# Block-sorted attention followed by a bilinear FFN: head pairs in row and column tiles, wide loads, a hand-written TensorE order, and x transposed by the DMA crossbar

## The chip, the cores and the metric

The kernel runs on one core of a Trainium2 chip. The metric is device time in microseconds, start to end. The kernel before takes 337.42 us (median of 3 runs, 336.62 to 338.02).

Engines are named as the profile names them: PE is TensorE (matmuls), PEld its weight loads, DVE VectorE, ACT ScalarE, POOL GpSimd (here mostly the issuer of casting loads: float32 in DRAM, bf16 on the chip), SP SyncE (issuer of stores and of crossbar transposes). PSUM is the memory that matmuls write to and that the other engines copy out of. A crossbar transpose is a DMA that transposes a tile on its way (DMA_TRANSPOSE in the profile). The granted clock is the share of full speed that PE is allowed.

## The reference, cut to what matters

```python
# q, k, v: [4 batches, 8 heads, 768, 64]; sort_net: [4, 8, 8, 8]
P = sort_net
for _ in range(5):                                   # Sinkhorn: rows, then columns
    P = exp(P - max(P)); P = P / (sum(P, -1) + 1e-9); P = P / (sum(P, -2) + 1e-9)
k_sorted = einsum('bhij,bhjcd->bhicd', P, k_b)       # mixes the 8 blocks of 96 rows
v_sorted = einsum('bhij,bhjcd->bhicd', P, v_b)
scores   = q_b @ k_sorted_b.T / sqrt(64)             # within each block of 96
attn     = softmax(scores) @ v_sorted_b              # [4, 8, 768, 64]
x   = attn.transpose(0, 2, 1, 3).reshape(3072, 512)
out = ((x @ w_a) * (x @ w_b)) @ w_out                # d_ff 1536; out 3072 x 512, float32
```

Arithmetic on the chip is bf16 with fp32 accumulation.

## The kernel before

One head at a time. Both k and v of a head go through one mixing matmul per 128 rows: the stationary operand is 128 x (64 of k + 64 of v), the moving one a 128 x 128 matrix `s_all` that spreads the 8 x 8 mixing matrix over the blocks.

```python
# loads: runs of 64 elements (256 bytes), cast to bf16, issued by POOL
for t, srct in enumerate((k, v)):
    sap = _ap(srct, (b * H + h) * S * D,
              [[D, CPG], [BLK * D, NB], [CPG * D, NCH], [1, D]])
    nc.gpsimd.dma_start(out=kv_b16[:, :, t, :], in_=sap)
# mixing: k and v of one head side by side, 128 columns
nc.tensor.matmul(mix_ps[:, ch, :], lhsT=kv_b16[:, half * 3 + ch, :, :],
                 rhs=s_all[:, bh, :], start=True, stop=True)
# ... copies to kvsT, v transposed on PE, then per half head:
#     scores -> exp (ACT) -> output matmul -> reciprocal and multiply (DVE) into x_b
# at the end of a batch: x transposed on PE, 2 x (96 x 128) to a PSUM tile, and copied
for i in range(NB):
    for fc2 in range(KA // 2):
        xt_ps = ps_big.tile([P, 2, BLK], BF16, tag="psb")
        # ... two transposes, then a copy to xT by DVE (i even) or ACT (i odd)
# mask times mixing matrix, for all 32 heads, on POOL
for g in range(4):
    nc.gpsimd.tensor_tensor(out=_ap(s_all, g * 8 * P, ...), in0=..., in1=..., op=ALU.mult)
# order of the source; the scheduler interleaves it
attention_batch(0, ...)
# ... the three weights are loaded here
for b in range(B):
    if b + 1 < B:
        attention_batch(b + 1)
    ffn_ab(2 * b); ffn_ab(2 * b + 1); ffn_out(2 * b); ffn_out(2 * b + 1)
```

The softmax here doesn't subtract the row's maximum and nothing guards it: scores larger than these inputs give would overflow.

Of the kernel before, what the change touches and what calls it, by code (L numbers as in the profile page):

```python
# [12 lines left out]
INT32 = mybir.dt.int32  # L13
# [11 lines left out]
def kernel(  # L25
# [12 lines left out]
    P = 128  # L38

# [4 lines left out]
    NTOK = B * S  # L44
# [4 lines left out]
    CPG = P // NB  # L49
    NCH = S // P  # L50
    KA = DMODEL // P
    KO = DFF // P
    D2 = 2 * D
    NBH = NB // 2

    const = ctx.enter_context(tc.tile_pool(name="const", bufs=1))
    sink = ctx.enter_context(tc.tile_pool(name="sink", bufs=1))
    persist = ctx.enter_context(tc.tile_pool(name="persist", bufs=1))

    kvb = ctx.enter_context(tc.tile_pool(name="kvb", bufs=6))  # L60
    qf = ctx.enter_context(tc.tile_pool(name="qf", bufs=5))
    att = ctx.enter_context(tc.tile_pool(name="att", bufs=5))
    xb = ctx.enter_context(tc.tile_pool(name="xb", bufs=2))
    ffo = ctx.enter_context(tc.tile_pool(name="ffo", bufs=2))

    ps_big = ctx.enter_context(tc.tile_pool(name="ps_big", bufs=3, space=bass.MemoryType.PSUM))
    ps_small = ctx.enter_context(tc.tile_pool(name="ps_small", bufs=1,
                                              space=bass.MemoryType.PSUM))
    ps_ffn = ctx.enter_context(tc.tile_pool(name="ps_ffn", bufs=2, space=bass.MemoryType.PSUM))

    ident = const.tile([P, P], BF16)
    make_identity(nc, ident)

    blkmask = const.tile([P, CPG, NB], BF16)
    nc.gpsimd.memset(blkmask, 1.0)
    nc.gpsimd.affine_select(
        out=blkmask, in_=blkmask, compare_op=ALU.is_ge, fill=0.0,
        base=0, pattern=[[-NB, CPG], [0, NB]], channel_multiplier=1,
    )
    nc.gpsimd.affine_select(  # L80
        out=blkmask, in_=blkmask, compare_op=ALU.is_ge, fill=0.0,
        base=(NB - 1), pattern=[[NB, CPG], [0, NB]], channel_multiplier=-1,
    )

    sel = const.tile([D, NB, P], BF16)
    nc.gpsimd.memset(sel, 0.0)
    for i in range(NB):
        nc.gpsimd.affine_select(
            out=_ap(sel, i * P, [[NB * P, D], [NB, CPG], [1, NB]]),
            in_=_ap(sel, i * P, [[NB * P, D], [NB, CPG], [1, NB]]),  # L90
            compare_op=ALU.not_equal, fill=1.0,
            base=-i, pattern=[[0, CPG], [-NB, NB]], channel_multiplier=1,
        )

    w_a_sb = persist.tile([P, KA, DFF], BF16)
    w_b_sb = persist.tile([P, KA, DFF], BF16)
    w_out_sb = persist.tile([P, KO, DMODEL], BF16)

    def load_weights(w_ap, w_sb, kk):
        src = w_ap.rearrange("(kc p) n -> p kc n", p=P)  # L100
        for kc in range(kk):
            nc.gpsimd.dma_start(out=w_sb[:, kc, :], in_=src[:, kc, :])

    xT = persist.tile([P, KA, NTOK], BF16)

    def load_q_pair(b, hp, qT_of):
        q_b16 = qf.tile([P, 2, NCH, D], BF16, tag="q_b16")
        nc.gpsimd.dma_start(
            out=q_b16,
            in_=q[b, 2 * hp:2 * hp + 2].rearrange("e (p c) d -> p e c d",  # L110
                                                  p=P))
        for e in range(2):
            q_ps = ps_small.tile([D, NCH, P], BF16, tag="pss")
            for c in range(NCH):
                nc.tensor.matmul(q_ps[:, c, :], lhsT=q_b16[:, e, c, :],  # L115
                                 rhs=ident, is_transpose=True)
            qTe = qf.tile([D, NCH, P], BF16, tag=f"qT{e}")
            if e == 0:
                nc.vector.tensor_copy(out=qTe, in_=q_ps)
            else:  # L120
                nc.scalar.copy(out=qTe, in_=q_ps)
            qT_of[2 * hp + e] = qTe

    def attention_batch(b, qT_of=None, skip_q=False):
        x_b = xb.tile([BLK, NB, H, D], BF16, tag="x_b")

        if qT_of is None:
            qT_of = {}
        for h in range(H):
            bh = b * H + h  # L130
            if h % 2 == 0 and not skip_q:
                load_q_pair(b, h // 2, qT_of)
            kv_b16 = kvb.tile([P, NCH, 2, D], BF16, tag="kv_b16")
            for t, srct in enumerate((k, v)):
                sap = _ap(srct, (b * H + h) * S * D,
                          [[D, CPG], [BLK * D, NB], [CPG * D, NCH], [1, D]])
                nc.gpsimd.dma_start(out=kv_b16[:, :, t, :], in_=sap)

            kvsT = kvb.tile([D2, NB, BLK], BF16, tag="kvsT")
            for half in range(2):  # L140
                mix_ps = ps_big.tile([D2, NCH // 2, P], FP32, tag="psb")
                for ch in range(NCH // 2):
                    nc.tensor.matmul(  # L143
                        mix_ps[:, ch, :],
                        lhsT=kv_b16[:, half * 3 + ch, :, :],
                        rhs=s_all[:, bh, :], start=True, stop=True)
                dst = _ap(kvsT, half * (NCH // 2) * CPG,
                          [[NB * BLK, D2], [CPG, NCH // 2], [BLK, NB],
                           [1, CPG]])
                srcp = _ap(mix_ps, 0,  # L150
                           [[(NCH // 2) * P, D2], [P, NCH // 2], [1, NB],
                            [NB, CPG]])
                if half == 0:
                    nc.scalar.copy(out=dst, in_=srcp)  # L154
                else:
                    nc.vector.tensor_copy(out=dst, in_=srcp)  # L156

            vs_ps = ps_small.tile([BLK, NB, D], BF16, tag="pss")
            for i in range(NB):
                nc.tensor.matmul(vs_ps[:, i, :], lhsT=kvsT[D:D2, i, :],  # L160
                                 rhs=ident[D:D2, D:D2], is_transpose=True)
            vs_sb = att.tile([BLK, NB, D + 1], BF16, tag="vs_sb")
            nc.gpsimd.memset(vs_sb[:, :, D:D + 1], 1.0)
            nc.vector.tensor_copy(out=vs_sb[:, :, 0:D], in_=vs_ps)  # L164

            qT = qT_of[h]
            eT = att.tile([BLK, NB, BLK], BF16, tag="eT")
            rec = att.tile([BLK, NB], FP32, tag="rec")
            for half in range(2):
                i0 = half * NBH  # L170
                sc_ps = ps_big.tile([BLK, NBH, P], FP32, tag="psb")
                for i in range(NBH):
                    qsl = _ap(qT, CPG * (i0 + i),
                              [[NCH * P, D], [P, NCH], [1, CPG]])
                    nc.tensor.matmul(sc_ps[:, i, 0:BLK],  # L175
                                     lhsT=kvsT[0:D, i0 + i, :], rhs=qsl,
                                     start=True, stop=True)
                nc.scalar.activation(out=eT[:, i0:i0 + NBH, :],  # L178
                                     in_=sc_ps[:, :, 0:BLK], func=AF.Exp,
                                     scale=float(scale))  # L180
                o_ps = ps_big.tile([BLK, NBH, P], FP32, tag="psb")
                for i in range(NBH):
                    nc.tensor.matmul(o_ps[:, i, 0:D + 1],  # L183
                                     lhsT=eT[:, i0 + i, :],
                                     rhs=vs_sb[:, i0 + i, :],
                                     start=True, stop=True)
                nc.vector.reciprocal(out=rec[:, i0:i0 + NBH],  # L187
                                     in_=o_ps[:, :, D])
                nc.vector.tensor_tensor(  # L189
                    out=x_b[:, i0:i0 + NBH, h, :], in0=o_ps[:, :, 0:D],  # L190
                    in1=_ap(rec, i0, [[NB, BLK], [1, NBH], [0, D]]),
                    op=ALU.mult)

        for i in range(NB):
            for fc2 in range(KA // 2):
                xt_ps = ps_big.tile([P, 2, BLK], BF16, tag="psb")
                for f in range(2):
                    fc = fc2 * 2 + f
                    nc.tensor.matmul(  # L199
                        xt_ps[:, f, :],  # L200
                        lhsT=x_b[:, i, 2 * fc:2 * fc + 2, :],
                        rhs=ident[0:BLK, 0:BLK], is_transpose=True)
# [4 lines left out]
                if i % 2 == 0:  # L207
                    nc.vector.tensor_copy(out=dst, in_=src)  # L208
                else:
                    nc.scalar.copy(out=dst, in_=src)  # L210
# [130 lines left out]
```

## Time and profile before

| stage of the kernel before | us |
|---|---|
| until the first FFN matmul | 69 |
| one batch period in the steady state (126.4 to 197.3, and to 268.2) | 70.9 |
| of it: a and b projections, 192 matmuls at 162 ns start to start | 31.2 |
| of it: output projection, 72 matmuls at 216 ns | 15.6 |
| of it: attention of the next batch (the rest) | 24.1 |
| last batch's FFN, no attention beside it (283.7 to 330.5) | 46.8 |

Start-to-start times here and below are differences of neighbouring start times in the trace; the busy time of a matmul in the profile is longer (329 ns against 162 for the a and b projections), so neighbours overlap.

The first view is the table by stages (windows) of the kernel before. Columns: the stretch in us, its length, busy us and instruction count of PE, PEld, DVE, ACT and POOL, granted PE clock, mean busy share of the DMA engines, GB/s.

```profile
0.00:68.00 68.00, 35.31 (x325) 28.23 (x326) 29.65 (x89) 19.53 (x38) 53.61 (x88) 1.00 1.07 123
126.40:142.00 15.60, 15.60 (x74) 6.94 (x72) 1.94 (x3) 1.75 (x3) 0.00 (x0) 1.00 0.22 84
142.00:197.30 55.30, 53.48 (x513) 33.89 (x514) 35.52 (x83) 31.45 (x61) 16.01 (x27) 1.00 0.55 46
283.70:314.90 31.20, 31.20 (x194) 18.79 (x192) 12.74 (x23) 11.96 (x25) 0.00 (x0) 1.00 0.03 9
```

PE is never idle in the output projection or in an a/b stage alone; where attention is interleaved (142 to 197.3) it is nearly full too, and in the first 68 us it is busy half of the time.

The next view is the groups of instructions for the x transpose of the kernel before: count, busy us and mean ns, then idle time before them and what ended it.

```profile
L210 ACT COPY xT<-xt_ps 128x192 bf16<-128x192 bf16 x32 | 23.7, 873 | 6.1 <-PE xt_ps L199 6.0
L208 DVE COPY xT<-xt_ps 128x192 bf16<-128x192 bf16 x32 | 23.6, 834 | 3.3 <-PE xt_ps L199 2.9
L199 PE MATMUL xt_ps<-ident,x_b 96*128 96x96 bf16 x128 | 15.3, 219 | 7.6 <-ACT xT L210 5.0 <-DVE xT L208 2.0
```

The lines of a timeline below hold start, length, engine, line, idle time before it and what released it.

```profile
49.68 0.58 PE L160 MATMUL vs_ps<-ident,kvsT 64*96 64x64 bf16 x5 [0.74 <-DVE kvsT L156]
...
51.20 0.53 PE L183 MATMUL o_ps<-vs_sb,eT 96*96 96x65 bf16 x4 [0.65 <-ACT eT L178]
...
52.78 0.53 PE L183 MATMUL o_ps<-vs_sb,eT 96*96 96x65 bf16 x4 [0.57 <-ACT eT L178]
53.12 0.83 PE L143 MATMUL mix_ps<-s_all,kv_b_593 128*128 128x128 bf16 x6
...
54.06 0.56 DVE L156 CAST kvsT<-mix_ps 128x384 bf16<-128x384 f32 x1
...
54.77 0.57 PE L160 MATMUL vs_ps<-ident,kvsT 64*96 64x64 bf16 x5 [0.81 <-DVE kvsT L156]
```

Each head is a chain: mixing, copy, scores, exponential, output, and only then the mixing of the next head. From 49.68 to 54.77 a head costs 5.1 us, in which PE, DVE and ACT are busy for 3.1, 2.2 and 1.5 us.

### The profile page before, as it was taken

What the parts mean: (1) busy time and instruction counts of PE and PEld (TensorE: products, weight loads), DVE (VectorE), ACT (ScalarE), POOL (GpSimd) and SP (SyncE); (2) the same over time, 40 slices, a digit from 0 to 9 for tenths busy, and PEclk for the clock granted to TensorE, in tenths of its full rate; (3) what the DMA queues carried; (4) which work ended last, traced back from release to release, by engine and by line L of the source; (5) the groups of instructions that cost most, each with busy time, mean ns of one, the idle gap of its engine ahead of it and who ended that gap; (6) DMA issues with size and microseconds to landing.
All of it is one profiled execution on the core that took longest, in us unless ns stands there. A gap on an engine that the chain in (4) does not pass through costs nothing.

```text
span 334.5 us, 5969 instructions
## 1 busy us (share of the span) xinstructions
PE 291.2 (87%) x2345; PEld 177.1 (53%) x2345; DVE 160.0 (48%) x376; ACT 136.5 (41%) x263; POOL 92.5 (28%) x154
## 2 busy tenths in 40 slices
PE   0356666689999799999998999999998999999995
PEld 0345444456666464466664554566665644665542
DVE  4413443567777741057678530366677410344300
ACT  2132222375555831156556521355647311433210
POOL 9899635963543000045431000120000000000000
PEclk9999999999999999999999999999999999999999
DMA  0909999997999001268973002450000012000022
GB/s 12 130 0 104 168 212 202 158 150 50 72 73 73 1 2 57 100 83 69 72 49 26 1 0 96 110 33 0 2 2 0 3 63 96 32 0 2 0 94 94
DMA packets 60940, 20.83 MB, mean 62 GB/s; under 512 B 51185, under 2 KB 56817, under 8 KB 60913
## 3 DMA queue, kind: packets, MB, share of 16 engines
q0 software_dynamic: 57408, 14.16, 44.6%
q1 hardware_dynamic: 3504, 6.30, 5.0%
q8 instruction: 18, 0.29, 0.4%
q14 instruction: 10, 0.07, 0.1%
HBM read 28.32 MB, written 6.29 MB: 103 GB/s over the span
## 4 chain that ended last, share of the span: by engine, by line
PE 74%; DMA 9%; POOL 6%; ACT 5%; DVE 3%; issue 1%; POOLq 0%; ACTq 0%
PE pb L278 19%; PE po L289 19%; PE pa L272 19%; ACT xT L210 4%; PE q_ps L115 4%; PE sc_ps L175 4%; DMA w_out_sb<-in_moe_w_out_dram 3%; PE o_ps L183 3%; POOL s_all L251 3%; PE mix_ps L143 3%; PE vs_ps L160 3%; DMA w_a_sb<-in_moe_w_a_dram 2%; PE xt_ps L199 2%; DMA q_b_786<-in_q_dram 1%; DMA kv_b_431<-in_v_dram 1%
## 5 line engine op out<-in xcount | busy, mean ns | idle before, releaser
L272 PE MATMUL pa<-xT,w_a_sb 128*128 128x384 bf16 x384 | 85.7, 329 | 0.0
L278 PE MATMUL pb<-xT,w_b_sb 128*128 128x384 bf16 x384 | 85.1, 329 | 0.0
L281 DVE TENSOR_TENSOR hT<-a_sb,pb 128x384 bf16<-128x384 bf16 x96 | 53.5, 557 | 50.2 <-PE pb L278 43.1
L276 ACT CAST a_sb<-pa 128x384 bf16<-128x384 f32 x96 | 46.9, 488 | 47.4 <-DVE hT L281 34.0
L289 PE MATMUL po<-w_out_sb,hT 128*128 128x512 bf16 x288 | 62.8, 379 | 0.0
L178 ACT ACTIVATE eT<-sc_ps 96x384 bf16<-96x384 f32 x64 | 31.1, 486 | 45.9 <-PE sc_ps L175 45.4
L289 PEld LDWEIGHTS <-hT 128*128 128x128 bf16 x288 | 28.2, 98 | 33.5
L272 PEld LDWEIGHTS <-w_a_sb 128*128 128x128 bf16 x384 | 35.0, 98 | 19.9 <-issue 0.2
L278 PEld LDWEIGHTS <-w_b_sb 128*128 128x128 bf16 x384 | 34.6, 98 | 20.0
L294 ACT COPY o_sb<-po 128x512 f32<-128x512 f32 x16 | 9.4, 585 | 56.3 <-PE po L289 56.3
L183 PE MATMUL o_ps<-vs_sb,eT 96*96 96x65 bf16 x256 | 25.0, 226 | 8.3 <-ACT eT L178 7.6
L183 PEld LDWEIGHTS <-eT 96*96 96x96 bf16 x256 | 19.4, 138 | 19.0 <-ACT eT L178 15.5
L189 DVE TENSOR_TENSOR x_b<-o_ps,rec 96x256 bf16<-96x256 f32 x64 | 27.2, 426 | 1.7
L296 DVE COPY o_sb<-po 128x512 f32<-128x512 f32 x8 | 5.5, 691 | 46.8 <-PE po L289 46.8
L175 PE MATMUL sc_ps<-qTe,kvsT 64*96 64x96 bf16 x256 | 27.3, 232 | 0.0
L210 ACT COPY xT<-xt_ps 128x192 bf16<-128x192 bf16 x32 | 23.7, 873 | 6.1 <-PE xt_ps L199 6.0
L208 DVE COPY xT<-xt_ps 128x192 bf16<-128x192 bf16 x32 | 23.6, 834 | 3.3 <-PE xt_ps L199 2.9
L160 PE MATMUL vs_ps<-ident,kvsT 64*96 64x64 bf16 x256 | 19.2, 221 | 6.2 <-DVE kvsT L156 5.3
L160 PEld LDWEIGHTS <-kvsT 64*96 64x96 bf16 x256 | 16.1, 137 | 14.8 <-ACT kvsT L154 7.0
L154 ACT CAST kvsT<-mix_ps 128x384 bf16<-128x384 f32 x32 | 15.3, 479 | 19.2 <-PE mix_ps L143 19.0
L164 DVE COPY vs_sb<-vs_ps 96x512 bf16<-96x512 bf16 x32 | 13.5, 423 | 20.0 <-PE sc_ps L175 12.0
L187 DVE RECIPROCAL rec<-o_ps 96x4 f32<-96x4 f32 x64 | 11.3, 177 | 24.6 <-PE o_ps L183 24.1
(213 smaller groups left out, 259.6 us busy)
## 6 DMA issues: line engine op xcount, KB each, us to landing
out_dram<-o_sb SPq DMA_DIRECT2D x24, 256.0 KB, 2.0
w_a_sb<-in_moe_w_a_dram POOLq DMA_DIRECT2D x4, 384.0 KB, 7.7
w_b_sb<-in_moe_w_b_dram POOLq DMA_DIRECT2D x4, 384.0 KB, 12.2
w_out_sb<-in_moe_w_out_dram POOLq DMA_DIRECT2D x12, 128.0 KB, 6.7
q_b_131<-in_q_dram POOLq DMA_DIRECT2D x1, 192.0 KB, 3.5
q_b_151<-in_q_dram POOLq DMA_DIRECT2D x1, 192.0 KB, 4.4
q_b_171<-in_q_dram POOLq DMA_DIRECT2D x1, 192.0 KB, 4.8
q_b_191<-in_q_dram POOLq DMA_DIRECT2D x1, 192.0 KB, 5.3
```

Source lines behind the costliest of these rows:

```text
L160: nc.tensor.matmul(vs_ps[:, i, :], lhsT=kvsT[D:D2, i, :], rhs=ident[D:D2, D:D2], is_transpose=True)
L175: nc.tensor.matmul(sc_ps[:, i, 0:BLK], lhsT=kvsT[0:D, i0 + i, :], rhs=qsl, start=True, stop=True)
L178: nc.scalar.activation(out=eT[:, i0:i0 + NBH, :], in_=sc_ps[:, :, 0:BLK], func=AF.Exp, scale=float(scale))
L183: nc.tensor.matmul(o_ps[:, i, 0:D + 1], lhsT=eT[:, i0 + i, :], rhs=vs_sb[:, i0 + i, :], start=True, stop=True)
L189: nc.vector.tensor_tensor(out=x_b[:, i0:i0 + NBH, h, :], in0=o_ps[:, :, 0:D], in1=_ap(rec, i0, [[NB, BLK], [1, NBH], [0, D]]), op=ALU.mult)
L208: nc.vector.tensor_copy(out=dst, in_=src)
L210: nc.scalar.copy(out=dst, in_=src)
L272: nc.tensor.matmul(pa, lhsT=w_a_sb[:, kc, m * P:(m + 1) * P], rhs=xT[:, kc, t0:t0 + TOK_CH], start=(kc == 0), stop=(kc == KA - 1))
L276: nc.scalar.copy(out=a_sb, in_=pa)
L278: nc.tensor.matmul(pb, lhsT=w_b_sb[:, kc, m * P:(m + 1) * P], rhs=xT[:, kc, t0:t0 + TOK_CH], start=(kc == 0), stop=(kc == KA - 1))
L281: nc.vector.tensor_mul(out=hT[:, m, :], in0=a_sb, in1=pb)
L289: nc.tensor.matmul(po, lhsT=hT[:, m, sub * P:(sub + 1) * P], rhs=w_out_sb[:, m, :], start=(m == 0), stop=(m == KO - 1))
```

## The change

The intent is to work on two heads at once. A pair's q transposes and its k and v mixing put the one head into the array's left 64 columns and the other into the right (column tiles); its scores put one head's 64 contraction rows above the other's (row tiles). Copies become twice as wide. A partition now holds 6 consecutive rows of the sequence, so loads read runs of 1536 bytes. The source interleaves the next batch's attention with the FFN steps, and PE's queue is filled in exactly that order. x is transposed by a crossbar DMA on the SP queue. POOL's mask work for batch 0 goes to DVE. FFN matmuls keep number and size. Weights come in fewer or differently cut loads, and the small steps that lead to the mask tile changed as well.

The diff, cut to its core:

```diff
-            nc.gpsimd.dma_start(out=kv_b16[:, :, t, :], in_=sap)
+        for name, t in (("k2", k), ("v2", v), ("q2", q)):
+            to = ld.tile([P, 2, W], BF16, tag=name, name=name)
+            nc.gpsimd.dma_start(
+                out=to, in_=_ap(t, (b * H + 2 * hp) * S * D, [[W, P], [S * D, 2], [1, W]]))
 ...
-                    nc.tensor.matmul(
-                        mix_ps[:, ch, :],
-                        lhsT=kv_b16[:, half * 3 + ch, :, :],
-                        rhs=s_all[:, bh, :], start=True, stop=True)
+        for c in range(NCH):
+            for e in range(2):
+                nc.tensor.matmul(
+                    mix[e * D:(e + 1) * D, c // 3, c % 3 * P:(c % 3 + 1) * P],
+                    lhsT=src2[:, e, c * D:(c + 1) * D],
+                    rhs=s_all[:, 2 * g + e], start=True, stop=True)
 ...
+                    nc.tensor.matmul(
+                        sc[:, e, i * BLK:(i + 1) * BLK],
+                        lhsT=kT[e * D:(e + 1) * D, blk * BLK:blk * BLK + P],
+                        rhs=qT[e * D:(e + 1) * D, blk], start=True, stop=True)
 ...
-                    nc.tensor.matmul(
-                        xt_ps[:, f, :],
-                        lhsT=x_b[:, i, 2 * fc:2 * fc + 2, :],
-                        rhs=ident[0:BLK, 0:BLK], is_transpose=True)
+        nc.sync.dma_start_transpose(
+            out=_ap(xT, g % HP * S, [[KA * S, P], [BLK, NB], [1, BLK]]),
+            in_=st[g, "xp"].rearrange("q i e d -> q (i e d)"))
 ...
+    with tc.manual_schedule(engines={mybir.EngineType.PE}):
 ...
+            spread(nc.vector, pc_ps, 0, 2)          # mask tile of batch 0, on DVE
+            spread(nc.vector, pc_ps, 2, 6)
+            for c in range(4):
+                load_ab(c)
+            for hp in range(HP):
+                load_pair(1, hp)
+            for g in range(1, 4):
+                spread(nc.gpsimd, p_col, g * 8, 8)  # the other batches', on POOL
 ...
+            for g in range(1, HP):
+                stage_q(g, ps0b, "B")
+            C0(0); C0(1); R0(0); O0(0); to_xT(0, ps0b, "B")
+            C0(2); R0(1); O0(1); to_xT(1, ps0b, "B")
+            C0(3); R0(2); O0(2); to_xT(2, ps0b, "B")
+            R0(3); O0(3); to_xT(3, ps0b, "B")
```

`C0` is k and v mixing of a pair, `R0` scores and v transpose, `O0` output and normalisation. In the loop, 16 such units (q and mixing; scores and v; output; x) are spread over the 30 FFN steps of a batch.

## The prediction

> **What bounds it now.** The timeline by windows has two regimes. (1) A preamble of 68 of 334.5 us, before the first FFN matmul, with PE busy half of it. Sinkhorn ends at 11.3 us; POOL then builds the mask tile s_all (4 x 2.74 us, to 24.5 us), and the k/v loads of most heads, queued behind it on POOL, are issued only after that, in 256-byte runs at about 125 GB/s. N=128 matmuls pace at 107 ns there, 56 after. (2) A PE-bound steady state of 70.9 us a batch (126.4 to 197.3 to 268.2): 31.2 us of a/b projections (192 matmuls, 162 ns start to start), 15.6 us of output projection (72 at 216 ns), and 24.1 us of attention. Of that about 7 us is the x transpose: its 32 small matmuls pace at 122-137 ns on average where 42 is usual, held by the 0.83-0.87 us copies to xT on DVE and ACT. The last batch runs without attention; a 4 us tail follows.
>
> **What changes.** FFN matmuls: same number and sizes, so 187 us stay. Their moving operand now has runs of 16 elements; before's score matmuls already read so and reach 45 ns at N=96, so I expect no loss.
>
> Attention on PE, per batch: 32 transposes and their copies go to the DMA crossbar (-7 us). Mixing doubles to 96 matmuls, q stays 48, but both in pairs of column tiles; scores 64 in pairs of row tiles; v transposes halve to 32. The before trace shows a row-tile pair overlapping: interleaved vs/sc matmuls come two in 45 ns. For column tiles nothing there tells; the Trainium skill ("TensorE: Matmul & The Clock Gate", Part 3) measured 2.38x for three. Estimate if pairs overlap: q 24x56, mix 48x56, scores 32x43, v 32x56, o 64x35 ns = 9.4 us, plus about 3-4 us of switching and waits on PSUM copies in the hand-written in-order PE stream: 13 us, against 24. If column tiles do not overlap, +4 us a batch. DVE and ACT stay near half busy (estimate 31 and 25 us of 60).
>
> Preamble: loads are issued from 0.8 us on (0.71 us each, as q loads now), in 1536-byte runs, so about 190 GB/s: batch 0 landed by 15 us. DVE makes batch 0's s_all, about 1.3 us. Then DVE is the slow engine, about 3.5-4 us a pair, plus three q copies: four pairs end near 36 us. The last x transpose by DMA is exposed: the skill ("Advanced Engine Details and Errata", X-Bar Transpose) gives 350-400 GB/s, 0.5 us for 192 KB; with the 2.0 us that output stores need to land, I take 4 us. First FFN matmul at 40 us (68 before). Weights and batch 1 follow at 200 GB/s, landed by about 42 us: just in time, perhaps a 1-2 us stall.
>
> **Sum.** 40 + 3x60 + 46.8 + 4 = 271 us span, about 273 us timed. Critical-path gains: 28 preamble, 33 attention.
>
> **Shows it right or wrong.** First FFN matmul at 36-46 us; batch period 57-64 us; q and mix start to start 28 ns mean (56 if no overlap); FFN 162 ns; DMA packets under a third of 60,940; x transposes landing in under 6 us, and no PE wait on xT at batch borders.
>
> **Would make it wrong.** A crossbar transpose of 10 us or more (four a batch, on one queue); POOL holding s_all for batch 1 behind 20 loads with 8 in flight, stalling the in-order PE; DVE/ACT order delaying FFN PSUM copies with 3 banks; strided FFN operand slower.
>
> Expected 273 us, 80% range 258 to 294; faster by over 2% 0.96, within 2% 0.02, slower 0.02.

## More of the kernel before

The transposes come in one bunch at the end of each batch, and PE and the copies wait for each other there. In PE's timeline one bunch lasts 7.1 us (177.99 to 185.08); 16 FFN matmuls run inside it, which need 2.6 us at 162 ns, so the bunch adds about 4.5 us to a batch.

## The result, and the profile after

The changed kernel takes 275.65 us (median of 4 runs, 274.61 to 276.25) against 337.25 us (4 runs) of the kernel before in the same rounds: ratio 0.8172, 95% interval 0.8149 to 0.8196. Ratios here are the mean time of one kernel's fast runs over that of the other's of the same rounds, so not quite the ratio of the medians quoted.

The stages of the changed kernel, in the same columns as above:

```profile
0.00:36.60 36.60, 15.84 (x312) 13.33 (x312) 23.10 (x76) 13.55 (x26) 20.81 (x33) 0.99 1.20 172
36.60:47.70 11.10, 1.44 (x3) 0.34 (x4) 0.02 (x1) 0.00 (x0) 8.96 (x8) 0.50 1.28 192
107.60:149.50 41.90, 41.85 (x482) 27.12 (x482) 24.47 (x49) 22.14 (x44) 0.00 (x0) 1.00 0.10 22
149.50:165.30 15.80, 15.75 (x87) 7.48 (x88) 3.47 (x7) 1.76 (x3) 0.00 (x0) 1.00 0.29 95
```

The steady state is full. Between 36.6 and 47.7 us, however, PE does three matmuls, the DMA engines are saturated (busy share 1.28), and the granted clock falls to half.

The chain of work that ended last, in order of time, shows where each batch's a/b stage starts:

```profile
107.56 1.30 PE pf L228 x8
...
165.28 1.30 PE pf L228 x8
...
223.00 31.20 PE pf L228 x192
```

With the first full FFN group at 47.76, the batches take 59.8, 57.72 and 57.72 us (107.56 - 47.76 and so on). The last FFN takes 46.75 us and the tail 4.65: together 274.4, the span. An FFN without attention is 46.8 us, so attention now costs 57.7 - 46.8 = 10.9 us a batch, where it cost 24.1.

Where the 13.2 us went can be read from the two traces, by adding up, over two batch periods of each (126.4 to 268.2 and 107.4 to 222.8 us), the time from each matmul's start to the next start:

| us a batch | before | changed |
|---|---|---|
| q transposes | 3.9 | 1.4 |
| k and v mixing | 2.8 | 3.1 |
| scores | 4.2 | 1.8 |
| v transposes | 2.9 | 1.8 |
| output | 3.6 | 2.1 |
| x transposes (4.5 with the FFN delay inside their bunch) | 3.4 | none |
| a and b projections beyond their 31.2 | 3.2 | 0.7 |

No single item carries the gain, and mixing gained nothing: it needs twice the matmuls.

The timeline at the end of the first stage, where the time is lost:

```profile
36.64 1.87 SPq L213 DMA_TRANSPOSE xT<-xp  x1
36.72 0.48 PE L228 MATMUL pf<-xT,w_a_sb 128*128 128x384 bf16 x1 [1.65 <-DVE xp L196]
...
39.58 0.48 PE L228 MATMUL pf<-xT,w_a_sb 128*128 128x384 bf16 x1 [2.38 <-DMA xT<-xp]
...
43.52 0.48 PE L228 MATMUL pf<-xT,w_a_sb 128*128 128x384 bf16 x1 [3.47 <-DMA xT<-xp]
...
47.76 0.48 PE L228 MATMUL pf<-xT,w_a_sb 128*128 128x384 bf16 x1 [3.76 <-DMA xT<-xp]
```

The first FFN group needs all four pairs' x, one matmul each. All attention of batch 0 is finished by 36.6 us, and then the four transposes come in one after another; the last, issued at 36.64, is there 11 us later. The next lines are the issues of transposes (count, median us from issue to landing) in the windows 24 to 50, 58 to 75 and 80 to 275 us, and the clock, in tenths, in 40 slices of the span (6.9 us each), from the page:

```profile
xT<-xp SPq DMA_TRANSPOSE x4, 10.1
...
xT<-xp SPq DMA_TRANSPOSE x2, 10.0
...
xT<-xp SPq DMA_TRANSPOSE x10, 2.8
...
PEclk9999965699999999999999999999999999999999
```

Six of the sixteen transposes are slow: the four of the first stage and the first two of the loop (10.4 and 9.5 us), beside which loads still run. The other ten land in 2.8 to 2.9 us, with no load packet starting while they move. In the loop nobody waits for any of them; only the first four stand on the path.

One pair's q transposes and mixing in the loop:

```profile
74.76 0.53 PE L131 MATMUL q_ps<-ident,q_234 128*64 128x128 bf16 x12
75.12 0.50 PE L145 MATMUL mix<-s_all,k_230 128*64 128x128 bf16 x12
75.45 0.50 PE L145 MATMUL mix<-s_all,v_232 128*64 128x128 bf16 x12
75.89 0.82 PE L228 MATMUL pf<-xT,w_a_sb 128*128 128x384 bf16 x4
```

Twelve matmuls of N=128 start within 0.34 us, 28 ns each. In the kernel before, such matmuls started 55 to 56 ns apart. This is the overlap of column tiles, of which the trace before said nothing.

### The profile page after: what moved, and what is told of

Read it like the earlier page. It is cut to its first block, busy times and chain, and to the rows that moved or that the text cites. A ratio compares the mean times of both kernels' runs of the same rounds, so it can differ in the third digit from the quotient of the medians.

```text
span 274.4 us, 5477 instructions
## 1 busy us (share of the span) xinstructions
PE 238.8 (87%) x2272; PEld 144.2 (53%) x2280; DVE 122.5 (45%) x268; ACT 98.5 (36%) x194; POOL 48.7 (18%) x67
## 3 DMA queue, kind: packets, MB, share of 16 engines
q0 software_dynamic: 18864, 14.16, 35.5%
## 4 chain that ended last, share of the span: by engine, by line
PE 85%; DMA 7%; POOL 3%; DVE 3%; issue 1%; ACT 0%; POOLq 0%; DVEq 0%; ACTq 0%
PE pf L228 46%; PE po L244 23%; PE mix L145 4%; DMA xT<-xp 4%; PE vs_ps L177 3%; PE o_ps L189 3%; DMA q_102<-in_q_dram 3%; PE sc L166 3%; PE q_ps L131 2%; DVE xp L196 1%; DVE vs_115 L179 1%; DVE rec L193 0%; ACT kT_106 L155 0%; POOL k_77 L78 0%; POOL v_88 L78 0%
## 5 line engine op out<-in xcount | busy, mean ns | idle before, releaser
L228 PE MATMUL pf<-xT,w_a_sb 128*128 128x384 bf16 x384 | 79.9, 330 | 11.3 <-DMA xT<-xp 9.6
L237 DVE TENSOR_TENSOR hT<-a_sb,pf 128x384 bf16<-128x384 bf16 x96 | 53.1, 553 | 78.1 <-PE pf L228 67.9
L228 PE MATMUL pf<-xT,w_b_sb 128*128 128x384 bf16 x384 | 78.8, 328 | 0.0
L236 ACT CAST a_sb<-pf 128x384 bf16<-128x384 f32 x96 | 46.0, 479 | 82.8 <-PE pf L228 51.6
L228 PEld LDWEIGHTS <-w_a_sb 128*128 128x128 bf16 x384 | 35.5, 98 | 30.4 <-issue 7.1
L196 DVE TENSOR_TENSOR xp<-o_ps,rec 96x512 bf16<-96x512 f32 x32 | 21.2, 684 | 0.5
L135 DVE COPY qT<-q_ps 128x768 bf16<-128x768 bf16 x16 | 8.8, 551 | 3.4 <-PE q_ps L131 3.4
L155 ACT CAST kT_106<-mix 128x384 bf16<-128x384 f32 x12 | 5.2, 482 | 14.3 <-PE mix L145 14.3
L170 ACT ACTIVATE eT_112<-sc 96x768 bf16<-96x768 f32 x12 | 9.1, 802 | 2.0 <-PE sc L166 1.9
L193 DVE RECIPROCAL rec<-o_ps 96x8 f32<-96x8 f32 x32 | 5.2, 185 | 8.7 <-PE o_ps L189 8.7
L170 ACT ACTIVATE eT_113<-sc 96x768 bf16<-96x768 f32 x10 | 7.5, 803 | 1.2 <-PE sc L166 1.2
L170 ACT ACTIVATE eT_114<-sc 96x768 bf16<-96x768 f32 x10 | 7.5, 802 | 0.9 <-PE sc L166 0.9
L155 ACT CAST kT_108<-mix 128x384 bf16<-128x384 f32 x10 | 4.3, 482 | 5.3 <-PE mix L145 5.3
L155 ACT CAST kT_107<-mix 128x384 bf16<-128x384 f32 x10 | 4.3, 482 | 5.1 <-PE mix L145 5.1
L258 POOL TENSOR_TENSOR s_all<-mask,p_col 128x1024 bf16<-128x1024 bf16 x3 | 5.9, 2000 | 0.0
```

The source lines that it names most:

```text
L135: nc.vector.tensor_copy(out=qT.rearrange("p i c t -> p c i t"), in_=q_ps.rearrange("p c (i t) -> p c i t", i=NB))
L155: nc.scalar.copy(out=d1, in_=s1)
L170: nc.scalar.activation(out=eT[:, hf, :, 0:HB], in_=sc[0:BLK, :, 0:HB], func=AF.Exp, scale=float(scale))
L196: nc.vector.tensor_tensor(out=_ap(xp, hf * NBH * 2 * D, [[NB * 2 * D, BLK], [D, 2], [2 * D, NBH], [1, D]]), in0=_ap(o_ps, 0, [[1024, BLK], ...
L228: nc.tensor.matmul(pf[:, 0:HW], lhsT=w_sb[:, kc, m * P:(m + 1) * P], rhs=_ap(xT, kc * S + t * 3 * CG, [[KA * S, P], [CG, 3], [BLK, NB], [1 ...
L236: nc.scalar.copy(out=a_sb, in_=pf[:, 0:HW])
```

## The experiments

Each experiment changes the changed kernel, unless it says otherwise. All gave correct results. Ratios are to the kernel before in the same rounds; the changed kernel's is 0.8172.

| run | time, us (4 runs; 5 for the mask run) | ratio | first full FFN group, us | loop period, us |
|---|---|---|---|---|
| changed kernel | 275.65 | 0.8172 | 47.8 | 57.72 |
| loads of batch 1 held back | 276.09 | 0.8159 | 39.5 | 57.72 |
| batch 0's x on PE | 266.27 | 0.7858 | 37.9 | 57.72 |
| all x on PE | 270.52 | 0.7985 | 38.6 | 59.1 |
| one column tile after the other | 277.26 | 0.8187 | 48.1 | 58.28 |
| column tiles kept apart | 293.46 | 0.8683 | 48.4 | 63.47 |
| narrow loads | 291.32 | 0.8616 | 52.8 | 57.72 |
| kernel before, mask on DVE | 337.34 | 0.9975 | 70.1 | 70.8 |
| earlier start | 261.07 | 0.7721 | 32.9 | 57.72 |
| one pair at a time | 276.23 | 0.8153 | 48.0 | 57.72 |
| scheduler's PE order | 273.01 | 0.8048 | 46.9 | 57.72 |

(The first full FFN group is dated by the matmul that needs the last pair's x, where the others came before it. In the scheduler's run q and most of the mixing of batch 1's first pair come before that matmul, which runs at 46.9, so its loop is further on by then than in the changed kernel. The kernel before itself has 69.0 and 70.9; it has two FFN chunks a batch, and its period is that of the batch.)

### Are the first transposes slow in themselves, or because of the loads beside them?

```diff
-            for hp in range(HP):
-                load_pair(1, hp)          # and load_out(c), before the first stage
+            # after the last to_xT of batch 0; each load's tile is first written
+            # with a few elements of xT, so the load has to wait for the transposes
+            # (w_out_sb's tiles likewise):
+            nc.gpsimd.tensor_copy(out=to[0:1, 0, 0:KA], in_=xTs[0][0:1, :, S - 1])
```

> The loads of batch 1 and of the output weights are held back until the last x transpose of batch 0 has landed; everything else is as in the changed kernel. Theory A (the transposes before the first FFN matmul are slow because each shares the DMA engines with queued loads, packet by packet): the fourth transpose lands in about 3 us instead of 11, PE's wait before the FFN shrinks from 11 us to about 3, and the first FFN group runs at about 40 us instead of 48. Theory B (crossbar transposes of one after another are slow in themselves, or the first ones are): landing stays near 11 us and the FFN still starts near 48. In both, PE then waits some 4 us for the late batch-1 loads, so the time under A is about 271 us, under B 280 or more.

```profile
36.74 1.12 PE L231 MATMUL pf<-xT,w_a_sb 128*128 128x384 bf16 x3 [1.65 <-DVE xp L199]
39.50 0.48 PE L231 MATMUL pf<-xT,w_a_sb 128*128 128x384 bf16 x1 [1.64 <-DMA xT<-xp]
39.77 1.48 PE L231 MATMUL pf<-xT,w_b_sb 128*128 128x384 bf16 x4
49.45 0.85 PE L134 MATMUL q_ps<-ident,q 128*64 128x128 bf16 x12 [8.19 <-DMA q<-in_q_dram]
```

(PE's timeline of this run.) With the engines free, the fourth transpose, issued at 36.7 as before, lets its matmul run at 39.50: 2.8 us instead of 11. The held loads then run beside the loop's first three transposes, and now those take 9.2 to 10.4 us where the changed kernel has 10.4, 9.5 and 2.8. Theory A holds, theory B falls. The total did not move, where 271 us were expected, since the held loads now made PE wait 8.2 us for batch 1's q, twice what I had expected: the wait was only moved.

The trace's DMA records show how the sharing goes. Each transpose is 768 packets of 256 bytes. In the changed kernel, between 36 and 46 us, 366 to 391 such packets and 367 to 376 packets of the loads (768 bytes written each) start in every 2 us: as many of the one as of the other. The four transposes take 5.0, 4.1, 4.1 and 4.2 us, strictly one after another, 39 to 48 GB/s; the fourth's first packet starts at 42.88, after a queue of two. So of its 11.1 us, 6.2 are queueing, 4.2 moving and 0.6 landing. In the run with held loads the third took 0.74 us and the fourth 1.15 us (265 and 171 GB/s). The Trainium skill ("DMA: Bandwidth & Descriptors", SWDGE vs HWDGE vs iDMA) says that software- and hardware-generated DMAs feed different queues inside each engine and that "the engine round-robins between them". The equal counts agree with that; whether the queues take turns singly or in groups, these counts don't tell. With 256-byte packets against 768-byte ones, equal turns leave the transpose a quarter of the bytes.

### What is the crossbar worth, in the first stage and in the loop?

```diff
+    def pe_xT(g, pool, tag):              # 8 transposes to one PSUM bank, two wide copies
+        x_ps = pool.tile([P, NB, BLK], BF16, tag=tag, name="x_ps")
+        for i in range(NB):
+            nc.tensor.matmul(x_ps[:, i], lhsT=xp[:, i], rhs=ident[0:BLK, 0:BLK],
+                             is_transpose=True)
+        nc.vector.tensor_copy(out=xT[:, g % HP, 0:HB], in_=x_ps[:, 0:NBH])
+        nc.scalar.copy(out=xT[:, g % HP, HB:2 * HB], in_=x_ps[:, NBH:NB])
 ...
-            C0(2); R0(1); O0(1); to_xT(1, ps0b, "B")       # and so on
+            C0(2); R0(1); pe_xT(0, ps0b, "B"); O0(1)       # one stage later, batch 0 only
```

> Batch 0 alone has x transposed on PE (8 transposes and two copies a pair), the other three batches keep the DMA crossbar. Theory A: the FFN starts at about 38 us instead of 48, then PE waits up to 3 us for the mask tile of batch 1, which POOL builds after all the batch-1 loads; and the half-speed clock from 36 to 52 us is gone (2 us). Time 265 to 268 us. Theory B says the same of the start, so this run does not tell A from B; it tells whether the crossbar costs or gains in this stage. If the loads, not the transposes, were what the FFN waited for, the time stays at 275.

266.27 us, ratio 0.7858: 9.4 us less than the changed kernel.

```profile
36.48 0.50 PE L222 MATMUL x_ps<-ident,xp 96*128 96x96 bf16 x4 [0.33 <-DVE xp L196]
37.94 1.44 PE L238 MATMUL pf<-xT,w_a_sb 128*128 128x384 bf16 x4 [0.96 <-ACT xT L225]
```

The FFN's first group runs whole at 37.94 instead of 47.76. The feared wait for the mask tile did not come. The clock still reads half speed from 35.5 to 42.4 us (35.9 to 53.0 in the changed kernel), and the part of the expectation that rested on it (2 us) did not come either: the first period is 59.8 us as before. The second run does the same in the loop:

```diff
-                            to_xT(g, psB, "B")
+                            pe_xT(g, psB, "B")
```

> All four batches have x transposed on PE. From the 42 ns of one small transpose in the kernel before, 32 a batch cost 1.4 us of PE, plus up to 1 us of waits on the copies: period 59 to 60 us a batch instead of 57.7, so about 5 us more than with the crossbar in the three later batches. If the crossbar is what made the attention cheap there, as the prediction put it at 7 us a batch, the three batches cost 20 us more and the time passes 285.

270.52 us, and a period of 59.1 us, 1.4 more than with the crossbar.

```profile
110.26 0.51 PE L222 MATMUL x_ps<-ident,xp 96*128 96x96 bf16 x8
110.60 0.81 PE L238 MATMUL pf<-xT,w_a_sb 128*128 128x384 bf16 x4
```

A pair's transposes take 0.34 us of PE (110.60 - 110.26), four pairs 1.37 us, and the period grows by just that: no wait is added. So the crossbar saves 1.4 us a batch in three batches and loses 9.4 us in the first: as used by the change, it is a net loss of about 5 us (275.65 against 270.52). The x transpose of the kernel before was mostly waiting: of the 4.5 us that its bunch adds to a batch, 32 transposes at 42 ns are 1.4. The rest goes when they come eight at a time between FFN steps, with two wide copies (0.36 and 0.48 us) for eight instead of a 0.83 to 0.87 us copy for two; which of the two counts for more, the spreading or the copies, was not separated.

### Do the column tiles overlap, and what is it worth?

```diff
-        for c in range(NCH):
-            for e in range(2):
+        for e in range(2):
+            for c in range(NCH):          # in stage_q and stage_mix
```

> Only the loop order of the q transposes and the mixing is swapped: all six matmuls of one column tile, then all six of the other, so that neighbours no longer use different column tiles. Theory A (pairs of column tiles overlap): start to start goes from 28 ns on average to about 56, 144 matmuls a batch cost 4 us more, three batches 12 us, the preamble 2 to 4 more: 289 to 292 us. Rival (the gain comes from fewer stages and the in-order stream, not from overlap): 275 to 278 us.

277.26 us: nearly nothing, so by its own wording the rival had won. The timeline says otherwise:

```profile
63.18 0.55 PE L131 MATMUL q_ps<-ident,q 128*64 128x128 bf16 x10
63.54 0.22 PE L145 MATMUL mix<-s_all,k 128*64 128x128 bf16 x1
63.57 0.22 PE L131 MATMUL q_ps<-ident,q 128*64 128x128 bf16 x1
63.60 0.22 PE L145 MATMUL mix<-s_all,k 128*64 128x128 bf16 x1
```

All 12 q transposes stand before the first mixing matmul in the program, yet mixing matmuls start between the last q transposes, 30 ns apart. The two column tiles run as two streams, one some matmuls ahead of the other: six q transposes of head 0, then k mixing of head 0, while the other tile is still at q of head 1. The experiment had not taken the overlap away; it needed another.

```diff
-                        def c_(g=g):       # q, k, v of both heads
+                        def c0_(g=g, tl=tl):   # q, k, v of head 0: one column tile
+                            tl["q"] = stage_q(g, psB, "B", heads=(0,))   # ... k, v alike
+                        def c_(g=g, tl=tl):    # an FFN step later: head 1, then the copies
+                            stage_q(g, psB, "B", heads=(1,), q_ps=tl["q"])  # ... k, v alike
-                        units += [c_, r_, o_, x_]
+                        units += [c0_, c_, r_, o_, x_]
```

> Swapping the order of neighbours did not take the overlap away: in the same-column run the first matmuls of the next stage on one column tile started between those of the stage before on the other, 25 to 30 ns apart. So in the FFN loop each pair's q transposes and mixing are now issued for head 0 (one column tile), then an FFN step on the whole array, then for head 1 (the other tile): nothing is left to overlap with. Overlap theory: 36 matmuls of a pair go from 28 ns start to start to 56, so 1.0 us more a pair, 4 us a batch, the period 57.7 to about 62 us, in all 12 to 14 us: 288 to 290 us. Rival (column pairs are worth little): under 279 us, the price of the added switches.

293.46 us, ratio 0.8683; the period is 63.47 us.

```profile
67.94 0.52 PE L132 MATMUL q_ps<-ident,q 128*64 128x128 bf16 x6
68.30 0.50 PE L149 MATMUL mix<-s_all,k 128*64 128x128 bf16 x6
68.64 0.50 PE L149 MATMUL mix<-s_all,v 128*64 128x128 bf16 x6
69.07 0.82 PE L234 MATMUL pf<-xT,w_a_sb 128*128 128x384 bf16 x4
```

Six matmuls now take the 0.34 us that twelve took. 144 matmuls a batch at 28 ns more are 4.0 of the 5.75 us by which the period grew. Added up from start to start as above, q and mixing cost 4.5 us more (the switches between stages included), the scores 0.85, and the a and b projections 0.4. The overlap of column tiles is real and worth at least 4 us a batch in this kernel. Against the kernel before it is worth less: without overlap q and mixing would take 9.0 us a batch, more than the 6.7 there, since mixing has twice the matmuls; with it they take 4.5.

### Loads: wide runs, and early issue

```diff
-            to = ld.tile([P, 2, W], BF16, tag=name, name=name)
+            to = ld.tile([P, NCH, 2, D], BF16, tag=name, name=name)
-            nc.gpsimd.dma_start(
-                out=to, in_=_ap(t, (b * H + 2 * hp) * S * D, [[W, P], [S * D, 2], [1, W]]))
+            for e in range(2):
+                nc.gpsimd.dma_start(
+                    out=to[:, :, e, :], in_=_ap(t, (b * H + 2 * hp + e) * S * D,
+                                                [[W, P], [D, NCH], [1, D]]))
```

> The changed kernel with its q, k and v loads cut into runs of 64 elements (256 bytes read, 128 written), one load per head, the same data and the same order of issue. If wide runs matter: q/k/v arrive at about 125 GB/s as in the kernel before instead of 190 to 200, batch 0 lands at 22 us instead of 17.5, everything queued behind it 10 us later, and PE waits for batch-1 tiles after the FFN has begun: 284 to 290 us. If only the early issue matters and not the width: 275 to 278.

291.32 us. From 10 to 20 us the DMA moved 120 GB/s instead of 201, mixing began at 25.5 us instead of 18.2, and PE waited 18.5 us in all for q tiles (11.2 in the changed kernel) and 7.3 us for a mask tile. POOL's timeline of this run says why the rate is what it is:

```profile
6.60 1.66 POOL L79 DMA_DIRECT2D k<-in_k_dram  x2
8.25 1.63 POOL L79 DMA_DIRECT2D v<-in_v_dram  x2
```

One load of 98,304 bytes (bf16) takes POOL 0.82 us to issue, 120 GB/s: just the rate that arrived. In the changed kernel a load of twice the bytes, with a third of the runs, takes 0.72 us. The engines were not what held them: from the first of these loads to the last, each landed 2.2 to 3.5 us after its issue ended, so no queue built up, while in the changed kernel that delay grew from 2.7 to 7.2 us. So the narrow runs, and the doubled number of loads, cost POOL's issue time first; the kernel before, at 0.80 us for the same size, has the same limit (98,304 / 0.80 = 123 GB/s). Wide runs are needed for the change to work: without them it loses 16 us.

But were the loads, or POOL's mask work before them, what made the first stage of the kernel before so long? I had said so. The next run changes the kernel before:

```diff
-        nc.gpsimd.tensor_tensor(
+        nc.vector.tensor_tensor(
             out=_ap(s_all, g * 8 * P, ...)
```

> The kernel before with one change: the mask tile s_all is built on DVE instead of POOL, so the k/v loads of batch 0 no longer queue behind 10.8 us of POOL work. If that queueing is what made the preamble long: FFN starts at 57 to 60 us instead of 68 to 70, time 326 to 329. If the narrow loads or the dependent stages bound it, the start moves by less than 4 us and the time stays above 333.

337.34 us, ratio 0.9975 (interval 0.9941 to 1.0009). The k/v loads of seven heads were now issued by 20.2 us (before, at 32.6), and the FFN still began at 70.1 us. PE's timeline:

```profile
36.48 0.57 PE L160 MATMUL vs_ps<-ident,kvsT 64*96 64x64 bf16 x5 [0.74 <-DVE kvsT L156]
...
39.86 0.83 PE L143 MATMUL mix_ps<-s_all,kv_b 128*128 128x128 bf16 x6
...
41.43 0.58 PE L160 MATMUL vs_ps<-ident,kvsT 64*96 64x64 bf16 x5 [0.74 <-DVE kvsT L156]
```

A head still takes 4.95 us (41.43 - 36.48), with its data long there. The run has a cost of its own: DVE spends 4 x 1.89 us on the mask, q copies wait for it, and the second head's mixing begins at 29.95 us instead of 28.29. That could hide a gain of some 1.7 us, not the 8 us and more that the theory needs. The loads and POOL were not the limit; the chains of dependent stages were: first the q transposes of batch 0, each waiting for the copy before it (13.2 to 25 us in the kernel before), with only the first head's mixing and first scores between them, then seven heads at 5.0 us.

### Is the first stage a chain, and what did the order do for it?

The version with batch 0's x on PE is taken, and its order changed:

```diff
-            C0(0); C0(1); R0(0); O0(0)
-            C0(2); R0(1); pe_xT(0, ps0b, "B"); O0(1)
-            C0(3); R0(2); pe_xT(1, ps0b, "B"); O0(2)
-            R0(3); pe_xT(2, ps0b, "B"); O0(3); pe_xT(3, ps0b, "B")
+            for g in range(HP):
+                C0(g); R0(g); O0(g); pe_xT(g, ps0b, "B")
```

> The version with batch 0's x transposed on PE (266.3 us, FFN from 37.9 us), its hand-written order in the first stage replaced by one pair after the other: mixing, scores, output, x transpose, then the next pair. Moving the mask tile off POOL left the kernel before where it was (337.3 us), with one head each 5.0 us in its first stage, PE waiting in turn for DVE's mixing copy, ACT's exponentials and the next load. Theory: the first stage is a chain of dependent stages, and the gain there is two heads per pass plus the mixing of later pairs issued ahead. Then this order costs 2 to 3 us a pair: FFN from 45 to 49 us, 274 to 278 us. Rival: loads pace the first stage; then 268 us or less.

276.23 us, FFN from 48.0 instead of 37.9.

```profile
22.32 1.04 PE L189 MATMUL o_ps<-vs,eT 96*128 96x65 bf16 x16 [0.78 <-DVE vs L179]
...
29.80 0.67 PE L189 MATMUL o_ps<-vs,eT 96*128 96x65 bf16 x16 [0.78 <-DVE vs L179]
...
36.82 0.67 PE L189 MATMUL o_ps<-vs,eT 96*128 96x65 bf16 x16 [0.78 <-DVE vs L179]
```

A pair takes 7.0 to 7.5 us; with the next pair's mixing issued ahead it takes 3.9 to 4.0 in the changed kernel (its output matmuls start at 23.36, 27.31 and 31.29), and two heads took 10 in the kernel before. So pairing and issuing ahead each give about 3 us a pair. In this slow order much of PE also paces at half speed (12 mixing matmuls in 0.64 us where the loop needs 0.34), which I did not separate; adding up the longer stages, I estimate that it is about 1.3 of the second 3 us. The heads of the kernel before also pace so.

Was it the pinning of the order, or the order of the source?

```diff
-    with tc.manual_schedule(engines={mybir.EngineType.PE}):
+    if True:
```

> The changed kernel with PE's order left to the scheduler. Its order in the FFN loop comes out the same as the hand-written one but for the first steps, since the source interleaves the stages already; in the first stage it mixes earlier. So if the hand-written order is worth something, it is only in the first 40 us: within 3 us of 275.6. If pinning matters, over 280.

273.01 us, ratio 0.8048 (0.8010 to 0.8086, apart from the changed kernel's 0.8149 to 0.8196). In the loop the scheduler arrives at the same order and the same 57.72 us, since the source already interleaves. In the first stage it begins mixing at 13.1 us instead of 18.2, and gives 3.5 us of that back in a wait for batch 1's mask tile. The pinned order is thus slightly worse, at a place that the last run mends.

### A version that beats both

```diff
             # batch 0's x on PE, as above, and:
-            for g in range(1, HP):
-                stage_q(g, ps0b, "B")
-            C0(0); C0(1); R0(0); O0(0)
-            C0(2); R0(1); pe_xT(0, ps0b, "B"); O0(1)
+            stage_q(1, ps0b, "B")
+            C0(0); C0(1); stage_q(2, ps0b, "B"); R0(0); O0(0)
+            C0(2); R0(1); stage_q(3, ps0b, "B"); pe_xT(0, ps0b, "B"); O0(1)
             # and POOL's mask tiles for batches 1 to 3 ahead of the loads of batch 1
```

> A version meant to beat both: batch 0's x transposed on PE as in the first of these experiments (266.3 us), and in the hand-written order the q transposes of pairs 2 and 3, which wait for loads until 14.6 and 17.5 us, come after the first mixing instead of before it; POOL builds the later mask tiles ahead of the batch-1 loads. Mixing starts at 13.5 us instead of 18.2, the FFN at 34 instead of 38: 262 us. If the loads of batch 0 or 1 are the true limit, PE waits on k, v or q tiles take the 4 us back: 265 to 267.

261.07 us (260.71 to 261.21), ratio 0.7721, 14.6 us less than the changed kernel.

```profile
13.09 0.85 PE L145 MATMUL mix<-s_all,k 128*64 128x128 bf16 x12
...
32.86 1.44 PE L238 MATMUL pf<-xT,w_a_sb 128*128 128x384 bf16 x4 [0.96 <-DMA k<-in_k_dram]
```

The last view names a load of k as what ended the 0.96 us wait before the FFN. That load landed at 34.3 us, after the matmul had started; ACT's copy to xT ended at 32.80, and the same 0.96 us wait stands in the first of these runs with ACT's copy as its end. So this wait is the copy. One wait for a load is left, 0.7 us for a q tile of batch 1.

In the changed kernel PE, executing in the written order, stood before the q transposes of pairs 2 and 3 until their loads landed (last at 17.5 us), with the first pair's mixing ready behind them. Moving these calls, and POOL's mask tiles, gave 5 us; the two were not separated.

## Why the prediction was right, and where it was wrong

The time (273 predicted, 275.65 measured) and its range were right, the direction too; but that it came so near was luck, two errors that cancel: 40 + 3x60 + 46.8 + 4 = 271 was measured as 47.8 + (59.8 + 57.7 + 57.7) + 46.8 + 4.6 = 274.4. The first FFN group came 7.8 us late, the three batches cost 4.8 us less than expected. (The very first FFN matmul, at 36.7 us, lies in the forecast of 36 to 46, but it needs one pair's x alone; the group could not go on.)

- **Attention on PE, 24 to 13 us a batch: right, the size even cautious.** Measured 10.9. The start-to-start times in the loop are 27.9 ns for q, 26.9 for mixing, 20.8 for scores, 57.3 for v and 32.1 for the output; times their counts 9.1 us, against the estimate of 9.4. Of the 3 to 4 us expected for switching and waits 1.8 were needed. That column tiles overlap was taken from the skill ("TensorE: Matmul & The Clock Gate", Part 3: 2.38x for three tiles, measured there with M=32 and N=512); this case agrees, with two tiles of 64 columns and N=128: 28 ns against 56, twice the pace.
- **"32 transposes and their copies go to the DMA crossbar (-7 us)": wrong as an attribution, and too large.** The bunch lasts 7.1 us, but 2.6 of them are FFN matmuls; it added 4.5. The crossbar did not take these away: the same transposes on PE, spread between FFN steps and copied in wide pieces, cost 1.4 us a batch. I counted a wait as if it were the work.
- **"The last x transpose by DMA is exposed ... I take 4 us": the mechanism right, the size wrong, 11.1 us.** This is the term that was most off. Alone a transpose lands in 2.8 us, so the estimate was ample for an idle DMA; 10.4 us of the 11.1 went into queueing and moving beside the loads. I had listed a slow crossbar as a risk, and had in the same paragraph the loads of weights and batch 1 running until 42 us on the same engines, without putting the two together. The forecast that every transpose would land in under 6 us failed for six of sixteen; that PE would not wait for xT at the later batch borders held. Attention itself ended at 36.6, where I had it ("near 36").
- **The cause of the long first stage: wrong.** I blamed POOL's mask work and the loads behind it; taking the mask off POOL changed nothing. It was a chain of one head at a time, 5.0 us each for seven of the eight. The change shortened that chain. I had DVE as the slow engine of a pair, 3.5 to 4 us; a pair took 3.9 to 4.0, but DVE was busy for only 2.9 of them, PE and ACT for 2.7 each: again a chain. So the forecast of 36 us for the four pairs held by luck, for a reason other than the one I gave. Wide loads are a condition for it (16 us when undone), not its cause.
- **FFN operand in runs of 16: right**, 162.7 ns mean start to start instead of 162 to 164.
- **Batch 1 "just in time": right in the changed kernel** (no wait on s_all or loads is left, as the FFN was late anyway); with the FFN moved to 39.5 us by holding loads, or to 32.9 in the last version, these waits do appear (8.2 and 0.7 us).
- **"DMA packets under a third of 60,940": wrong**, 35,193. The crossbar's own 256-byte packets, 12,288 of them, were not in my count; the 22,905 others are still more than a third of 60,940 (20,313).

## What to carry to other kernels

A transfer that is fast when alone can stand on the critical path at the moment when the DMA engines are full: ask of each new DMA what shares its engines then, and use different means in the first stage and in the loop if need be. A long first stage of a software pipeline can be a chain, as here; find what one pass of it takes and issue the next pass's first step ahead, before blaming loads. When an operation looks expensive in a profile, separate its own time from the waits around it before crediting its removal.

## What the Trainium skill lacked or had wrong

- "Advanced Engine Details and Errata", X-Bar Transpose (TRN2), says "TRN2 transpose DMAs are as fast as regular DMAs" and expects 350-400 GB/s. Here a 192 KB SBUF-to-SBUF transpose moved at 165 to 171 GB/s with no load beside it (once at 265, when it was queued behind another), while ordinary output stores of 256 KB on the same queue moved at about 315 (0.82 us); beside saturating loads it moved at 39 to 48 GB/s, in 256-byte packets that got as many turns as the loads' 768-byte ones. The turn-taking can be read in "DMA: Bandwidth & Descriptors", but its Rules for kernel authors say that a transpose next to ordinary DMAs "needs nothing"; that held here for the result, not for the time.
- "TensorE: Matmul & The Clock Gate", Part 3, has matmuls start and end in program order, "strict FIFO, no reordering". In the run with one column tile after the other, mixing matmuls of one column tile started at 63.54 and 63.60 us, before the q transpose at 63.63 us that precedes them in the program on the other column tile: in this trace the two column tiles advance independently.
- "DMA: Bandwidth & Descriptors" has no figure for POOL's issue time of a casting load. Here it was 0.72 us for 256 runs of 1536 bytes and 0.82 us for 768 runs of 256 bytes, which capped the narrow loads at 120 GB/s.
